# Moving stores of zeros to other places in the order of a backward attention kernel

## The chip, the cores and the metric

The kernel runs on one core of one Trainium2 chip. The metric is device time in microseconds (us); five executions of the kernel before took 283.5 to 284.99 us, with a median of 283.81 us. A sixth execution was profiled.

## What is computed

The program computes one layer's output and all gradients for a decode step: attention over the last 1024 positions of a cache of 4096, beside a gated feed-forward block.

```python
B, Sq, D = 4, 1, 512
Hq, Hkv, Sk, Dh = 32, 8, 4096, 128
W = min(4096, max(256, Sk // 4))          # 1024: only these positions are attended to
k = jnp.repeat(k_cache[:, :, Sk - W:, :], rep, axis=1)
v = jnp.repeat(v_cache[:, :, Sk - W:, :], rep, axis=1)
p = _softmax(jnp.einsum("bhqd,bhkd->bhqk", q, k) * (Dh ** -0.5), axis=-1)
return x + _A_ref(xn, A_k_cache, A_v_cache, A_wq, A_wo) + _B_ref(xn, B_w_gate, B_w_up, B_w_down)
_out, _vjp = jax.vjp(_f, A_x, A_k_cache, A_v_cache, A_wq, A_wo, B_w_gate, B_w_up, B_w_down)
return (_out0, *[jnp.asarray(_g) for _g in _grads])
```

The gradients of the two caches (`out_2` for k, `out_3` for v) have the full shape of 4 x 8 x 4096 x 128. Three quarters of each is zero, because positions 0 to 3071 are not attended to. These zeros have to be written to memory: 2 caches x 32 (batch, head) regions = 64 regions of 768 KB, 50 MB in all, out of 81 MB that the kernel writes.

## The kernel before, in words

The feed-forward block comes first. The eight kv heads then go in four groups of two (`NT = 4`, `t` = 0 to 3). For each group the code makes the scores of k (`scores(t, 0)`), the softmax, the scores dP of v (`scores(t, 1)`), then the gradient of the scores, dS (`softmax_d`), the rows of the output and of dq (`odq`), and sums over the weights (`fin`). While that goes on, the large outputs are made in small pieces from a queue `bg`, of which `tick(n)` takes n: `dvdk(t, 0)` gives 16 pieces of dv, `dvdk(t, 1)` 16 pieces of dk, `dw(t)` the pieces of the weight gradients.

**Pieces and stage tiles.** A piece of dv or dk (lines 532 to 543) is one matmul into PSUM (`kv_ps`, line 537), and a copy of it by ScalarE (line 99) or VectorE (line 101) into a stage tile of 1 MB. Eight pieces (jj = 0 to 7) fill one tile, for one head g; with the eighth the tile is stored, by a DMA that SyncE (SP) issues. So a group has four stage tiles, in the order dv g=0, dv g=1, dk g=0, dk g=1. The pool `stage` has three buffers. The last tile of a group, dk g=1, takes the buffer of that group's first, dv g=0, and its first copy waits until the store of dv g=0 has landed.

**DMA queues.** Stores of results go out in order on SP's queue. Stores of zeros go out on ScalarE's queue (line 311): `zeros(n)` issues a DMA for n regions, at most 4 in one, all from one small tile of zeros. A region is 64 pieces of 12 KB. Each such issue is tied to stand behind the latest copy of ScalarE (lines 312 and 313), so that its place among ScalarE's copies is where the call stands. Loads for group t + 2 go out on GpSimd's queue (`load_next`, lines 291 to 297): first v and k of the group's first head, then `wo`, `wq`, k and v of its second, each as soon as the tile that it replaces has been read.

**Places of the zeros.** `zeros` is called in the feed-forward block (2 and 4 regions, line 751), three times in `scores` of each group (4 each, line 411: in the middle of the second half of k's scores and of both halves of v's), in group 0 also between the two (2, line 768), and in the last two groups after `softmax_d`, whose input dP is then done (4, line 771). The call at line 786 would issue what is left; nothing is left by then. A semaphore that a DMA counts up is shared with earlier DMAs of SP and ScalarE in turn (eight of them), and an issue waits for the DMA that had it before.

Of the kernel before, what the change touches and what calls it, by code (L numbers as in the profile page):

```python
# [18 lines left out]
def kernel(  # L19
# [41 lines left out]
    GP = 2  # L61
    NT = G // GP
# [28 lines left out]
    def evac(out, in_, n, half=False, eng=None):  # L91

        eng = "dve" if half else eng or ("act" if chain else None)
        ca, cd = (190 + n) / 1.2, (120 + (n / 2 if half else n)) / 0.96
        if eng is None:
            eng = "act" if load["act"] + ca <= load["dve"] + cd else "dve"
        load[eng] += ca if eng == "act" else cd
        if eng == "act":
            last.append(nc.scalar.copy(out=out, in_=in_))  # L99
            return last[-1]  # L100
        return nc.vector.tensor_copy(out=out, in_=in_)  # L101

    def store(eng, out, in_, kind, apart):

        d = eng.dma_start(out=out, in_=in_)
        for k in apart:
            tc.declare_no_dep(d.ins, group=k, reason="stores write disjoint parts of the outputs")
        tc.add_to_no_dep_group(kind, d.ins)
        return d
# [166 lines left out]
    def load_w(t):  # L276
        eng = nc.gpsimd if t else nc.sync
        pool = wpool[t % 2]
        wo_t[t] = pool.tile([P, HG, D], BF16, name="wo_sb", tag="wo")
        eng.dma_start(out=wo_t[t][:], in_=wo_v[t])  # L280
        wq_t[t] = pool.tile([P, ND, CW], BF16, name="wq_sb", tag="wq")
        eng.dma_start(out=wq_t[t][:], in_=wq_v[t])

    def load_kv(t, k, g):
        d_, src, nm = ((k_t, A_k_cache, "kb"), (v_t, A_v_cache, "vb"))[k]
        tl = kvpool[(GP * t + g) % (2 * GP)].tile([P, J, Dh], BF16, name=nm, tag=nm)
        (nc.gpsimd if GP * t + g > GP else nc.sync).dma_start(out=tl[:].rearrange("p j d -> p (j d)"),
                          in_=src[:, t * GP + g, K0:Sk, :].rearrange("b (m j) d -> m b (j d)", j=J))
        d_[(t, g)] = tl
# [12 lines left out]
    def zeros(n):  # L302


        zs = ztile[0:P:P // ZP, :]
        while n > 0 and zruns:
            og, r = zruns[0]
            w = min(n, B * G - r, GP * 2)
            zsrc = bass.AP(tensor=zs.tensor, offset=zs.offset, ap=[list(zs.ap[0]), [0, w], [1, ZW]])
            zdst = og.rearrange("b g s d -> (b g) s d")[r:r + w, 0:K0, :].rearrange("r (m j) d -> m r (j d)", m=ZP)  # L310
            z = store(nc.scalar, zdst, zsrc, "zeros", ["rest", "zeros"])
            tc.add_manual_dep(z.ins, last[-1].ins.name,
                              mybir.DependencyInfo(mybir.DependencyClass.NoSync, mybir.DependencyReason.DATA))
            n -= w
            zruns[0][1] += w
            if zruns[0][1] == B * G:
                zruns.popleft()
# [4 lines left out]
    def tick(n):  # L322
        for _ in range(min(n, len(bg))):
            bg.popleft()()
# [57 lines left out]
    def masks(t):  # L382
        for k, nm in enumerate(("do", "q")):
            mr = attw.tile([P, GP, NQ, Dh], BF16, name=nm + "mr", tag=nm + "mr", bufs=1)
            for g in range(GP):
                nc.gpsimd.tensor_tensor(out=mr[:, g], in0=st[t]["r4"][:, k, :].unsqueeze(1).broadcast_to([P, NQ, Dh]),  # L386
                                        in1=msk[:, :, g].unsqueeze(2).broadcast_to([P, NQ, Dh]), op=ALU.mult)
            st[t][nm] = mr
# [137 lines left out]
    def dvdk(t, k):  # L526
        src, mr, og = st[t][("P", "dS")[k]], st[t][("do", "q")[k]], (out_3, out_2)[k]
        nm = ("dv", "dk")[k]
        for g in range(GP):
            held = {}  # L530

            def piece(g, jj, held):
                if jj == 0:
                    held["stg"] = stage.tile([P, NQ, JQ, Dh], BF16, name="stg_" + nm, tag="stg")
                stg = held["stg"]
                mps = ps_w.tile([P, NQ, Dh], FP32, name="kv_ps", tag="w")
                nc.tensor.matmul(mps[:].rearrange("p q d -> p (q d)"), lhsT=src[:, jj, :],  # L537
                                 rhs=mr[:, g].rearrange("p q d -> p (q d)"), start=True, stop=True)
                evac(stg[:, :, jj, :], mps[:], 512)
                if jj == JQ - 1:  # L540
                    store(nc.sync, out=og[:, t * GP + g, K0:Sk, :].rearrange("b (m j) d -> m b (j d)", j=J),
                          in_=stg[:].rearrange("p q j d -> p (q j d)"), kind="rest",
                          apart=["zeros", "rest"])

            for jj in range(JQ):
                bg.append(lambda g=g, jj=jj, held=held: piece(g, jj, held))
# [209 lines left out]
    with tc.tile_pool(name="stage", bufs=3, reuse_waits="tile") as stage, \  # L756
            tc.tile_pool(name="wodd", bufs=1, reuse_waits="tile") as wodd:
        wpool.append(wodd)
        kvpool.append(wodd)
        load_w(1)  # L760
        for k in range(2):
            load_kv(1, k, 1)
        for t in range(NT):
            if t == 0:
                pre(t, {})
            masks(t)
            scores(t, 0, {})
            zeros(2 if t == 0 else 0)
            scores(t, 1, softmax(t))
            d1, d2 = softmax_d(t)  # L770
            zeros(4 if t >= NT - 2 else 0)
            if t + 1 < NT:
                pre(t + 1, {0: [d1], 2: [d2]})
            else:
                tick(2)
                d1()
                tick(6)
                d2()
                tick(2)
            odq(t)  # L780
            fin(t)
            load_next(t)
            tick(len(bg))
            dw(t)
        tick(len(bg))
        zeros(2 * B * G)


        acc_r = kvp.tile([P, 2, ND, B, RB], FP32, name="acc_r", tag="kb")
        nc.vector.tensor_copy(out=acc_r[:], in_=acc[:].unsqueeze(4).broadcast_to([P, 2, ND, B, RB]))  # L790
        fin_ps = []
        for o in range(2):
            f_ps = ps_w.tile([P, ND, P], FP32, name="f_ps", tag="w")
            for c in range(ND):
                nc.tensor.transpose(f_ps[:, c, :], acc_r[:, o, c].rearrange("p b r -> p (b r)"), ident_f[:])
            fin_ps.append(f_ps[:])
        acc_o, acc_d = fin_ps[0].rearrange("p c d -> p (c d)"), fin_ps[1].rearrange("p c d -> p d c")

        def adj(x):
            return x[:].rearrange("p (d c) -> p d c", c=ND)  # L800

        out_b = kvp.tile([P, D], BF16, name="out_b", tag="vb")
        nc.vector.tensor_tensor(out=out_b[:], in0=acc_o, in1=x_b[:], op=ALU.add)
        nc.sync.dma_start(out=out_0.rearrange("b s d -> (b s) d"), in_=out_b[0:P:RB, :])

        s1 = const.tile([P, 1], FP32, name="s1")
        nc.vector.reduce_sum(out=s1[:], in_=acc_d, axis=AX.XY)
        pr = kvp.tile([P, D], FP32, name="pr", tag="vb")
        s2 = const.tile([P, 1], FP32, name="s2")
        nc.vector.tensor_tensor_reduce(out=adj(pr), in0=acc_d, in1=adj(xn_f), scale=1.0, scalar=0.0,  # L810
                                       op0=ALU.mult, op1=ALU.add, accum_out=s2[:])
        nm1 = const.tile([P, 1], FP32, name="nm1")
        nc.vector.tensor_scalar(out=nm1[:], in0=s1[:], scalar1=-1.0 / D, scalar2=None, op0=ALU.mult)
        nm2 = const.tile([P, 1], FP32, name="nm2")
        nc.vector.tensor_scalar(out=nm2[:], in0=s2[:], scalar1=-1.0 / D, scalar2=None, op0=ALU.mult)
        nc.vector.scalar_tensor_tensor(out=adj(pr), in0=adj(xn_f), scalar=nm2[:, 0:1], in1=acc_d,
                                       op0=ALU.mult, op1=ALU.add)
        nc.vector.tensor_scalar(out=pr[:], in0=pr[:], scalar1=nm1[:, 0:1], scalar2=rstd[:, 0:1],
                                op0=ALU.add, op1=ALU.mult)
        dx_b = kvp.tile([P, D], BF16, name="dx_b", tag="kb")  # L820
        nc.vector.tensor_tensor(out=dx_b[:], in0=pr[:], in1=dy_b[:], op=ALU.add)
        nc.sync.dma_start(out=out_1.rearrange("b s d -> (b s) d"), in_=dx_b[0:P:RB, :])
# [30 lines left out]
```

## Time and profile before

| What | Value |
|---|---|
| Median of five executions | 283.81 us |
| Profiled execution | 284.25 us |
| Its span (first to last instruction) | 282.5 us |
| Busy: PE, DVE, ACT, POOL | 76%, 56%, 41%, 20% |
| DMA, mean over the span | 397 GB/s, 112.15 MB |
| Share of ScalarE's queue, SP's queue, GpSimd's queue in the DMA engines' span | 42.3%, 39.0%, 15.2% |
| Stores of zeros: 15 of 3072 KB and 2 of 1536 KB, issue to landing | 19.0 and 18.4 us (median) |
| Stores of dv tiles, 8 of 1024 KB, issue to landing | 19.8 us (median) |

PE is TensorE, DVE VectorE, ACT ScalarE and POOL GpSimd. "SPq" and "ACTq" are the parts of SP and ScalarE that issue DMAs. The share of busy time is a mean over stretches with different limits, so it doesn't say what a change at one place is worth. The chain of waits is followed back from the last instruction to what released each step.

### The profile page before, as it was taken

The page shows a single profiled execution, that of the slowest core. Times are in us where ns is not written, and L with a number is a line of the kernel's source. Part 1 is how long each engine was busy: PE and PEld are TensorE (multiplying, and loading weights), DVE is VectorE, ACT ScalarE, POOL GpSimd, SP SyncE. Part 2 cuts the span into 40 slices and gives each one's busy share as a digit, 9 for nine tenths or more (in the row PEclk, how much of TensorE's full clock was granted, in tenths as well). Part 3 has the DMA queues.
Part 4 walks back from the last instruction along what each step waited for, and adds up shares of the span by engine and source line. Part 5 has one row for each costly group of instructions (what it writes and reads, how often), then busy time and mean ns, then how long its engine had stood idle before and what let it go on. Part 6 is the DMA issues. An engine that isn't in the chain of part 4 may idle for free.

```text
span 282.5 us, 7190 instructions
## 1 busy us (share of the span) xinstructions
PE 215.9 (76%) x3132; PEld 140.5 (50%) x3132; DVE 159.6 (56%) x336; ACT 115.6 (41%) x214; POOL 56.0 (20%) x56
## 2 busy tenths in 40 slices
PE   1978977987769789967894499786954996878950
PEld 0856854745445565534572265444642754526520
DVE  6955644654457557645583237546752465367691
ACT  1321643454336237535421335455303363571550
POOL 3890003130100534020006060110050201102000
PEclk9985997799798999999599559999896699799795
DMA  7999999999999999999999979999999769999995
GB/s 237 442 394 431 426 397 402 409 418 418 425 424 422 424 422 415 419 427 423 428 423 412 400 209 364 430 425 425 425 422 426 314 255 409 434 418 429 422 412 222
DMA packets 19407, 112.15 MB, mean 397 GB/s; under 512 B 1440, under 2 KB 5040, under 8 KB 10416
## 3 DMA queue, kind: packets, MB, share of 16 engines
q10 hardware_dynamic: 4384, 50.34, 42.3%
q1 hardware_dynamic: 12304, 44.58, 39.0%
q0 software_dynamic: 2688, 16.78, 15.2%
q8 instruction: 24, 0.39, 0.5%
q14 instruction: 7, 0.06, 0.0%
HBM read 30.68 MB, written 81.01 MB: 395 GB/s over the span
## 4 chain that ended last, share of the span: by engine, by line
PE 49%; DMA 23%; DVE 17%; ACT 4%; issue 3%; POOL 2%; ACTq 0%; DVEq 0%
DMA out_dram<-stg_dv 18%; PE T_ps L399 10%; PE kv_ps L537 6%; PE S_ps L404 5%; DMA out_dram<-osb_g 5%; PE dwo_ps L556 3%; DVE T_sb L101 3%; PE acc_ps L213 3%; PE wgT_ps L742 3%; PE dwq_ps L568 2%; POOL P_x L417 2%; PE woT_ps L338 2%; PE dwg_ps L715 2%; ACT stg_dk L99 2%; PE wqT_ps L595 2%
## 5 line engine op out<-in xcount | busy, mean ns | idle before, releaser
L101 DVE COPY T_sb<-T_ps 128x1024 bf16<-128x1024 bf16 x64 | 43.8, 690 | 38.3 <-PE T_ps L399 38.0
L99 ACT CAST stg_dk<-kv_ps 128x512 bf16<-128x512 f32 x40 | 22.0, 588 | 52.4 <-PE kv_ps L537 37.1
L99 ACT CAST stg_dv<-kv_ps 128x512 bf16<-128x512 f32 x57 | 30.4, 591 | 30.1 <-PE kv_ps L537 30.1
L537 PE MATMUL kv_ps<-qmr,dS_x 128*128 128x512 bf16 x64 | 22.5, 432 | 14.2 <-ACT stg_dk L99 12.4
L537 PE MATMUL kv_ps<-domr,P_x 128*128 128x512 bf16 x64 | 23.6, 444 | 5.4 <-POOL P_x L417 4.8
L101 DVE CAST stg_dk<-kv_ps 128x512 bf16<-128x512 f32 x24 | 16.1, 686 | 14.5 <-PE kv_ps L537 14.4
L399 PE MATMUL T_ps<-ident,kb 128*128 128x128 bf16 x256 | 24.2, 235 | 0.0
L399 PEld LDWEIGHTS <-kb 128*128 128x128 bf16 x256 | 19.2, 107 | 8.9 <-issue 6.4
L386 POOL TENSOR_TENSOR domr<-r,msk 128x512 bf16<-128x512 bf16 x8 | 8.2, 1041 | 77.0 <-DVE r L379 77.0
L99 ACT CAST osb_g<-dwg_ps 128x512 bf16<-128x512 f32 (+1 forms) x28 | 14.3, 538 | 18.9 <-PE dwg_ps L715 9.4
L399 PE MATMUL T_ps<-ident,vb 128*128 128x128 bf16 x256 | 21.4, 226 | 0.0
L399 PEld LDWEIGHTS <-vb 128*128 128x128 bf16 x256 | 16.6, 102 | 7.2 <-issue 5.6
L99 ACT CAST osb_o<-dwo_ps 128x512 bf16<-128x512 f32 x25 | 14.5, 587 | 10.6 <-PE dwo_ps L556 9.9
L404 PE MATMUL S_ps<-T_sb,dom 128*32 128x256 bf16 x128 | 12.7, 387 | 7.8 <-DVE T_sb L101 7.3
L417 POOL TENSOR_TENSOR P_x<-P_b,bmsk 128x1024 bf16<-128x1024 bf16 x4 | 7.6, 1893 | 54.1 <-ACT P_b L465 54.1
L101 DVE COPY woT<-woT_ps 128x1024 bf16<-128x1024 bf16 x16 | 11.0, 689 | 12.0 <-PE woT_ps L338 12.0
L99 ACT CAST osb_q<-dwq_ps 128x512 bf16<-128x512 f32 x25 | 14.2, 587 | 8.4 <-PE dwq_ps L568 7.8
L595 PEld LDWEIGHTS <-wq_sb 128*128 128x128 bf16 x128 | 9.0, 103 | 14.7 <-issue 13.0
L338 PE MATMUL woT_ps<-ident,wo_sb 128*128 128x128 bf16 x128 | 12.6, 253 | 2.6 <-DVE stg_dv L101 1.9
L338 PEld LDWEIGHTS <-wo_sb 128*128 128x128 bf16 x128 | 10.8, 116 | 7.1 <-issue 6.1
L101 DVE COPY wqT<-wqT_ps 128x1024 bf16<-128x1024 bf16 x16 | 11.0, 688 | 5.6 <-PE wqT_ps L595 5.5
L101 DVE COPY wgT<-wgT_ps 128x1024 bf16<-128x1024 bf16 x14 | 9.7, 692 | 7.6 <-PE wgT_ps L742 7.6
(214 smaller groups left out, 402.6 us busy)
## 6 DMA issues: line engine op xcount, KB each, us to landing
out_dram<-ztile ACTq DMA_DIRECT2D x15, 3072.0 KB, 19.0
out_dram<-stg_dv SPq DMA_DIRECT2D x8, 1024.0 KB, 19.8
out_dram<-stg_dk SPq DMA_DIRECT2D x8, 1024.0 KB, 13.2
kb<-in_A_k_cache_dram POOLq DMA_DIRECT2D x5, 1024.0 KB, 17.8
vb<-in_A_v_cache_dram POOLq DMA_DIRECT2D x5, 1024.0 KB, 25.0
out_dram<-osb_o SPq DMA_DIRECT2D x8, 512.0 KB, 14.0
out_dram<-osb_q SPq DMA_DIRECT2D x8, 512.0 KB, 16.9
out_dram<-osb_g SPq DMA_DIRECT2D x8, 448.0 KB, 15.2
```

Source lines behind the costliest of these rows:

```text
L99: last.append(nc.scalar.copy(out=out, in_=in_))
L101: return nc.vector.tensor_copy(out=out, in_=in_)
L213: nc.tensor.matmul(ps[:, c, :], lhsT=lf(c), rhs=rhs, start=(k == 0), stop=(k == len(terms) - 1))
L338: nc.tensor.transpose(wT_ps[:, i, c, :], wo_sb[:, 2 * h2 + i, c * P:(c + 1) * P], ident[:])
L386: nc.gpsimd.tensor_tensor(out=mr[:, g], in0=st[t]["r4"][:, k, :].unsqueeze(1).broadcast_to([P, NQ, Dh]), in1=msk[:, :, g].unsqueeze(2).bro ...
L399: nc.tensor.transpose(T_ps[:, jj, :], blks[(t, g)][:, q * JQ + jj, :], ident[:])
L404: nc.tensor.matmul(ps[b * RG:(b + 1) * RG, :], lhsT=lf[:, b, s * RG:(s + 1) * RG], rhs=T_sb[:, :, b], start=(g == 0 and q == 0), stop=(g = ...
L417: eng.tensor_tensor(out=dst[:].rearrange("p j (m b) -> p (j m) b", b=B), in0=src[:].unsqueeze(2).broadcast_to([P, WQ, B]), in1=bmsk[:].uns ...
L537: nc.tensor.matmul(mps[:].rearrange("p q d -> p (q d)"), lhsT=src[:, jj, :], rhs=mr[:, g].rearrange("p q d -> p (q d)"), start=True, stop= ...
L556: nc.tensor.matmul(mps[:], lhsT=X[:].rearrange("p h d -> p (h d)")[:, g * rep + i:CW:HG], rhs=dyz[:], start=True, stop=True)
L595: nc.tensor.transpose(wT_ps[:, i, c, :], wq_sb[:, c, h * Dh:(h + 1) * Dh], ident[:])
L742: nc.tensor.transpose(wT_ps[:, i, c, :], wsb[:, c, fc * P:(fc + 1) * P], ident[:])
```

## The change

Stores of zeros are issued in other places. The number of regions is the same, 64. A new call stands where the first piece of dk g=1 takes its stage tile, the tile that waits for dv g=0: 2 regions in group 1 and 3 in group 2. In exchange the call after `softmax_d` issues 2 regions instead of 4 in group 2, and 1 instead of 4 in group 3. There are 19 issues instead of 17.

```diff
             def piece(g, jj, held):
                 if jj == 0:
                     held["stg"] = stage.tile([P, NQ, JQ, Dh], BF16, name="stg_" + nm, tag="stg")
+                    if (k, g) == (1, GP - 1) and 0 < t < NT - 1:
+                        zeros(2 if t == 1 else 3)
                 stg = held["stg"]
...
             d1, d2 = softmax_d(t)
-            zeros(4 if t >= NT - 2 else 0)
+            zeros({NT - 2: 2, NT - 1: 1}.get(t, 0))
             if t + 1 < NT:
                 pre(t + 1, {0: [d1], 2: [d2]})
```

The order of instructions in the built program shows two further things. In groups 1 and 2 the new issue stands on ScalarE's queue between the last copy into dk g=0 and the first copy into dk g=1. And on GpSimd's queue the loads for group 3, which were issued in the order `wo`, `wq`, k, v, now come as `wq`, k, v, `wo`. The orders of TensorE and VectorE and of SP's stores are the same.

## The prediction

> **What bounds the kernel now.** I read the page's rows of DMA throughput first, because 112 MB have to pass.
>
> ```profile
> span 282.5 us, 7190 instructions
> ...
> DMA  7999999999999999999999979999999769999995
> GB/s 237 442 394 431 426 397 402 409 418 418 425 424 422 424 422 415 419 427 423 428 423 412 400 209 364 430 425 425 425 422 426 314 255 409 434 418 429 422 412 222
> ```
>
> A slice is 7.06 us. Where nothing starves it, the DMA moves about 425 GB/s. It has two holes, slices 23 and 24 (162 to 176 us) and 31 and 32 (219 to 233 us); each misses about 0.65 of a slice, 4.6 us. The chain of waits in order of time tells what comes before each hole:
>
> ```profile
> 131.50 27.02 DMA out_dram<-stg_dv
> ...
> 158.61 0.59 ACT stg_dk L99
> ...
> 190.45 24.49 DMA out_dram<-stg_dv
> ...
> 215.04 0.59 ACT stg_dk L99
> ...
> 275.69 0.69 DVE dx_b L821
> ```
>
> Columns are start, us, what. The whole kernel from 131 us on hangs on two landings of a dv tile (at 158.6 and 215.0). After each comes a chain of compute: 31.8 us to the next dv store, and after the second 61.4 us to the last vector instruction (276.4). ScalarE's timeline shows the copies that waited, the last tiles of groups 1 and 2:
>
> ```profile
> 149.80 1.07 ACT L99 CAST stg_dk<-kv_ps 128x512 bf16<-128x512 f32 x2 [3.84 <-PE kv_ps L537]
> 158.61 1.56 ACT L99 CAST stg_dk<-kv_ps 128x512 bf16<-128x512 f32 x3 [7.74 <-DMA out_dram<-stg_dv]
> ...
> 207.57 0.59 ACT L99 CAST stg_dk<-kv_ps 128x512 bf16<-128x512 f32 x1 [3.79 <-PE kv_ps L537]
> 215.04 1.07 ACT L99 CAST stg_dk<-kv_ps 128x512 bf16<-128x512 f32 x2 [6.88 <-DMA out_dram<-stg_dv]
> ```
>
> So ScalarE stands still for 7.74 and 6.88 us. The table by stretches shows the first hole:
>
> ```profile
> 158.00:162.00 4.00, 2.75 (x19) 1.76 (x18) 1.38 (x2) 2.35 (x5) 0.00 (x0) 0.50 0.98 414
> 162.00:166.00 4.00, 3.71 (x76) 3.00 (x76) 1.29 (x5) 0.87 (x2) 2.37 (x5) 0.50 0.44 117
> 166.00:171.00 5.00, 5.00 (x42) 2.81 (x41) 2.67 (x4) 2.80 (x5) 2.07 (x3) 0.69 0.99 277
> 171.00:176.00 5.00, 5.00 (x57) 2.80 (x56) 3.42 (x6) 3.04 (x6) 0.00 (x0) 1.00 1.01 416
> ```
>
> The last three columns are TensorE's granted clock, the DMA's share and GB/s. At the end the stores decide, by SP's timeline:
>
> ```profile
> 271.25 2.34 SPq L105 DMA_DIRECT2D out_dram<-osb_q  x2
> ...
> 276.41 0.54 SPq L822 DMA_DIRECT2D out_dram<-dx_b  x1
> ```
>
> The last vector instruction ends at 276.4, but the trace's last packets of osb_q run until 280.82, and the packets of dx_b, behind them in SP's queue, at 278.8. The span ends 1.66 us after the last packet.
>
> Counting the trace's packets by queue and size gives the prices (16 DMA engines; us of one packet: 12 KB 0.460, 8 KB 0.309, 4 KB 0.159, 2 KB 0.084):
>
> ```
> us               SP 8K/4K/2K    ACT 12K   POOL 8K/4K
> 192 to 196          0/0/118        120       0/0
> 150.9 to 158.6    222/0/2           18     133/0
> 171.15 to 214.94  312/256/512      910     256/130
> 262 to end        311/256/512      204       0/0
> ```
>
> **What the Trainium skill says.** "DMA: Bandwidth & Descriptors", section "Queues, rings and completion order": each DMA engine goes round the queues that have work, a packet from each. The trace agrees: 118 small packets of SP beside 120 of 12 KB from ScalarE in 4 us. A zero that waits beside a store thus costs that store 0.46 us per packet and engine. The same page, "Why a DMA increments its semaphore by 16 and not by 1": a DMA has landed when its slowest engine has. Here by 152 us 116 packets of 8 KB of the 128 of dv g=0 had started, yet it landed at 158.5. "TensorE: Matmul & The Clock Gate", part 1 on the HAM clock gate: the clock halves after an idle window of about 3.4 us. Here it was at half from 213.47 to 223.71, around a pause of 5.92 us, and at full through a pause of 1.81 us at 97.7.
>
> **The change, part by part.**
>
> *Two regions in group 1.* 128 packets, 8 for each engine, issued when ScalarE is free at 150.87. Their semaphore's earlier store, osb_o issued at 114.66, landed at 129.83, so nothing holds the issue. ScalarE's queue still has zeros until about 153, so the new ones follow. On the slowest engine the last osb_q landed at 152.53; from there to 158.5 its 8 packets of dv (2.5 us), about 3 zeros (1.4) and 8 of the loads (2.5) make 6.4 us. Now 8 zeros fit in between, 5 more: 5 x 0.46 = +2.3 us. Bounds: 0.9 if the zeros come only for the last 2 packets, 3.7 if all 8 come on top. I take +2.4: this wait becomes about 10 us, and all that is queued behind the copy (ScalarE's copies, TensorE's PSUM buffers, `fin`, the next scores) starts that much later.
>
> *The loads.* `wq` goes first, as soon as its last transposes are done (160.75 before) instead of behind `wo`'s issue (163.63). With the wait 2.4 longer it is issued at 163.2, the same moment as `wo` before. The load that now comes last, `wo`, is wanted at 191.78 + 2.4 = 194.2; the last load landed at 190.47. If that cover were gone, TensorE's pause of 5.92 us would take it.
>
> *The landing in group 2.* From 171.15 the DMA is never idle. The packets until the landing sum to (312 x 0.309 + 256 x 0.159 + 512 x 0.084 + 910 x 0.46 + 256 x 0.309 + 130 x about 0.25) / 16 = 44.4 us, against 43.8 passed. After: SP's stores come 2.4 us later, at 173.55. The loads have run alone for 2.4 us more, at the 45 packets a us of 166 to 171, so some 108 x 0.309 / 16 = 2.1 us of them are already done. The cut from 4 regions to 2 counts little: of the fourth store of zeros 142 packets had passed before the landing and 128 are left, 14 x 0.46 / 16 = 0.4 us. Landing: 173.55 + 43.8 - 2.1 - 0.4 = 214.8, i.e. -0.2 us. So what the first wait adds, the second gives back: it shrinks from 6.88 to about 4.3. Bounds of this shift: -2.5 to +2.4 (nothing given back).
>
> *Three regions in group 2.* Issued at about 210.6, when ScalarE's queue has packets anyway: none on the landing. Afterwards ScalarE's queue carries one region more than before, 64 x 0.46 / 16 = 1.8 us, into a hole of 4.6 us. Cost nothing; without the hole 1.8. The two added issues (0.61 us each) lie in ScalarE's waits.
>
> *One region for four in group 3.* 192 packets fewer, 192 x 0.46 / 16 = 5.5 us. Up to 262 us ScalarE sent 820 of this group's 1024; now there are 832, so SP has the DMA alone from there. Its own packets cost (311 x 0.309 + 256 x 0.159 + 512 x 0.084) / 16 = 11.2 us, which ends before the compute does. Then dx_b, issued at 276.41, sets the end: first packet 0.86 us later (as osb_o at 226.52, first packet 227.38), 277.3, and 1.66 more, 279.0 instead of 282.5: -3.5 us. Bounds: -2 if osb_q still drains at 277 to 279, -4.
>
> Sum: -0.2 - 3.5 = -3.7. The profiled execution, 284.25 us (1.75 around the span), becomes 280.5; the median lies 0.44 lower: **280.1 us**, its own range 278.5 to 282.
>
> **The rivals.**
>
> *The clock stays up.* If the second wait leaves TensorE less than the idle window (5.92 - 2.6 = 3.3 us), the half clock until 223.7 may not come. Groups of 8 transposes took 0.85 us there against 0.45: some 1.7 us less on the chain, 278.4 us. Against it: the clock was also halved at 135 us without such a pause.
>
> *Nothing given back.* The landing in group 2 moves with its issue: +2.4 - 3.5 = -1.1, 282.7 us, no change. For it: the loads alone, in `wq`'s 2 KB rows, moved 277 GB/s, so the extra time may move less.
>
> *Slower.* At 150.9 us the zeros delay stores and loads together. The first wait takes the full 8 x 0.46 = 3.7; the loads, pushed back as far, run 3.7 us longer beside osb_q, which then goes at 17 instead of 29 packets a us: 44 packets, +1.5 us at the second landing. 283.81 + 3.7 + 1.5 - 3.5 = 285.5 us. It decides once the shift at the second landing passes +4.9. Against it: the hole at 162 to 166, 117 GB/s, takes 3 us of such delay.
>
> That the issue comes too late, behind the waiting copy, is excluded by the program's order.
>
> **How the numbers follow.** Own forecast 0.46, clock 0.20, nothing given back 0.22, slower 0.12. Half a per cent, 1.4 us, is about what a measurement of this kernel can tell from no change: below 282.4 and above 285.2. The first two are faster, and a third of the third (0.07): 0.73. Same 0.15, slower 0.12. The range reaches from 277.0, below the clock's case by a larger tail gain, to 284.5, above the third case by a tail of only -2; beyond it lies mainly the slower case.
>
> **What would show it.** Group 1's wait on stg_dv about 10 us instead of 7.74; group 2's about 4 instead of 6.88; the first hole, 162 to 166, partly filled; the second filled by 1.8 us; the last packets near 277, with dx_b the last. The prediction is wrong if group 2's landing stands above 217, or if osb_q still ends after 280.

## The result and the profile after

The change makes no measurable difference. The kernel before took 284.44 us (median of 71 executions beside the runs below), the changed kernel 285.23 us (median of 36). The ratio is 1.0011, with a 95% interval of 0.9992 to 1.0031. The forecast was 280.1 us, faster. All ratios below are to the kernel before on the same chip and leave disturbed executions out, so they differ slightly from the quotient of two medians.

The changed kernel was profiled twice. The first profiled execution took 286.63 us (before: 284.25). Its page shows that the holes are still there:

```profile
span 284.9 us, 7191 instructions
...
DMA  7999999999999999999999989999999658999965
GB/s 237 435 413 424 422 400 420 406 414 429 424 425 427 421 422 416 425 429 421 423 426 424 419 278 361 427 426 426 427 416 428 273 234 353 422 435 418 421 285 218
```

A slice is now 7.12 us, counted from 0. The first hole (slices 23 and 24: 278 and 361 where before had 209 and 364) is a little shallower. The second (273, 234, 353) has become wider: against 425 GB/s it misses 0.98 of a slice, 7 us, where before missed 4.6. The region more that was forecast for it has not filled it. The chain of waits in order of time (start us, us, what) has the same two landings, both later:

```profile
130.09 32.78 DMA out_dram<-stg_dv
...
162.99 0.70 DVE stg_dk L101
...
195.69 24.75 DMA out_dram<-stg_dv
...
220.53 0.70 DVE stg_dk L101
...
281.54 0.69 DVE dx_b L823
```

The first landing takes 32.78 us from its issue instead of 27.02, and the second 24.75 instead of 24.49: it wasn't shortened. ScalarE's timeline shows the two new issues (ACTq) and the copies that wait:

```profile
148.76 0.61 ACTq L105 DMA_DIRECT2D out_dram<-ztile  x1
149.02 0.59 ACT L99 CAST stg_dk<-kv_ps 128x512 bf16<-128x512 f32 x1
162.97 1.56 ACT L99 CAST stg_dk<-kv_ps 128x512 bf16<-128x512 f32 x3 [13.36 <-DMA out_dram<-stg_dv]
...
211.68 0.63 ACTq L105 DMA_DIRECT2D out_dram<-ztile  x1
220.54 1.56 ACT L99 CAST stg_dk<-kv_ps 128x512 bf16<-128x512 f32 x3 [8.28 <-DMA out_dram<-stg_dv]
```

The waits grew from 7.74 to 13.36 us and from 6.88 to 8.28 us. The stretches around the first hole, in the columns of the table shown of before (the last three are TensorE's clock, DMA share and GB/s):

```profile
158.00:162.00 4.00, 0.00 (x0) 0.00 (x0) 0.00 (x0) 0.00 (x0) 0.00 (x0) 0.50 1.01 421
162.00:166.00 4.00, 1.48 (x10) 1.04 (x10) 1.38 (x2) 1.56 (x3) 0.95 (x2) 0.50 0.82 342
166.00:171.00 5.00, 4.71 (x85) 3.62 (x84) 1.34 (x5) 1.66 (x3) 2.27 (x4) 0.50 0.87 274
171.00:176.00 5.00, 5.00 (x42) 2.87 (x40) 2.41 (x4) 2.57 (x5) 1.19 (x2) 0.62 0.97 338
```

From 158 to 162 us no engine computes, while the DMA moves 421 GB/s. At the end, SP's timeline shows what was forecast:

```profile
277.12 1.50 SPq L105 DMA_DIRECT2D out_dram<-osb_q  x2
...
282.26 0.54 SPq L824 DMA_DIRECT2D out_dram<-dx_b  x1
```

The last packets of the execution are now those of `dx_b`, at 283.56 us; 2.6 us pass from the last vector instruction (282.24) to the end of the span, where before had 6.1 us (276.38 to 282.48).

### The profile page after: what moved, and what is told of

Its sections match the earlier page's. It is cut to its first block, busy times and chain, and to the rows that moved or that the text cites. A ratio compares the mean times of both kernels' runs of the same rounds, so it can differ in the third digit from the quotient of the medians.

```text
span 284.9 us, 7191 instructions
## 1 busy us (share of the span) xinstructions
PE 213.3 (75%) x3132; PEld 138.4 (49%) x3132; DVE 158.9 (56%) x336; ACT 115.5 (41%) x214; POOL 55.9 (20%) x56
## 4 chain that ended last, share of the span: by engine, by line
PE 44%; DMA 29%; DVE 17%; ACT 3%; issue 3%; POOL 2%; ACTq 0%; DVEq 0%; SPq 0%
DMA out_dram<-stg_dv 20%; PE T_ps L399 10%; PE kv_ps L539 7%; PE S_ps L404 6%; DMA out_dram<-osb_d 6%; DVE T_sb L101 4%; DMA out_dram<-ztile 3%; PE dwo_ps L558 3%; PE acc_ps L213 3%; PE dwq_ps L570 2%; POOL P_x L417 2%; PE wqT_ps L597 2%; DVE stg_dk L101 2%; PE wgT_ps L744 1%; DVE wqT L101 1%
## 5 line engine op out<-in xcount | busy, mean ns | idle before, releaser
L597 PE MATMUL wqT_ps<-ident,wq_sb 128*128 128x128 bf16 x128 | 11.0, 230 | 20.4 <-DVE stg_dk L101 17.5
L399 PEld LDWEIGHTS <-kb 128*128 128x128 bf16 x256 | 20.1, 111 | 11.1 <-issue 8.7
L399 PE MATMUL T_ps<-ident,kb 128*128 128x128 bf16 x256 | 25.1, 242 | 0.0
L399 PEld LDWEIGHTS <-vb 128*128 128x128 bf16 x256 | 16.3, 101 | 6.9 <-issue 5.0
L558 PE MATMUL dwo_ps<-dyz,od_x 128*128 128x512 bf16 x32 | 13.6, 461 | 0.2 <-ACT osb_o L99 0.2
```

The source lines that it names most:

```text
L399: nc.tensor.transpose(T_ps[:, jj, :], blks[(t, g)][:, q * JQ + jj, :], ident[:])
L558: nc.tensor.matmul(mps[:], lhsT=X[:].rearrange("p h d -> p (h d)")[:, g * rep + i:CW:HG], rhs=dyz[:], start=True, stop=True)
L597: nc.tensor.transpose(wT_ps[:, i, c, :], wq_sb[:, c, h * Dh:(h + 1) * Dh], ident[:])
```

## The experiments

The "price" of a place below is the ratio of a kernel with zeros there, less the ratio of the kernel that only lacks them at the end. One per cent is 2.84 us. The interval of a difference is worked out as the root of the two squared half widths.

### The end: regions left out

Two regions are taken from group 3's call and never written (`drop2`), or three (`drop3`).

```diff
-            zeros(4 if t >= NT - 2 else 0)
+            zeros({NT - 2: 4, NT - 1: 2}.get(t, 0))     # drop3: NT - 1: 1
...
-        zeros(2 * B * G)
```

> The kernel before with 2 regions fewer after softmax_d of group 3, and these 2 issued nowhere: they stay unwritten, so this is the worth of taking 2 regions out of the end, without the price of another place. Theory (from there the end is set by the store of dx_b): the part from the last vector instruction to the end shrinks from 6.1 to 2.7 us, the waits of groups 1 and 2 stay at 7 to 8: 281 us, ratio 0.985 to 0.991. Rival (the end does not hang on these zeros): ratio 0.996 to 1.002.

> As the kernel with 2 unwritten regions, but with 3 (group 3 issues 1 after softmax_d, as in the changed kernel). Theory: no more is gained than with 2, because dx_b sets the end either way: ratio 0.985 to 0.991, and the gap to the kernel with group 2's call alone, 1.0054, is what 3 regions in group 2 cost, about 1.6%. Rival (each region is worth its DMA time, 1.84 us, since the DMA's total is the bound): 0.65% below the kernel with 2 unwritten regions.

Measured: 0.9855 [0.981, 0.9901] and 0.9854 [0.9807, 0.99]. So emptying the end is worth 1.45%, 4.1 us (forecast: 3.5), and the third region adds nothing to the second. SP's timeline of the kernel with two regions left out ends as that of the changed one does:

```profile
271.45 1.48 SPq L105 DMA_DIRECT2D out_dram<-osb_q  x2
273.09 1.15 SPq L803 DMA_DIRECT2D out_dram<-out_b  x1
276.57 0.54 SPq L821 DMA_DIRECT2D out_dram<-dx_b  x1
```

`dx_b` goes out at 276.57 us, as before (276.41), but the last packet passes at 278.23 instead of 280.82. What is gained here has to be paid for at the place the zeros are moved to.

### Group 1 alone

Only the call in group 1, with two regions, and group 3 short of two; with four regions; and, for the part that the changed order of group 3's loads plays, that order alone. (Both kernels with group 1's call have this order too: `wq`, k, v, `wo`.)

```diff
                     held["stg"] = stage.tile([P, NQ, JQ, Dh], BF16, name="stg_" + nm, tag="stg")
+                    if (k, g) == (1, GP - 1) and t == 1:
+                        zeros(2)                         # g1_four: zeros(4)
...
-            zeros(4 if t >= NT - 2 else 0)
+            zeros({NT - 2: 4, NT - 1: 2}.get(t, 0))     # g1_four: {NT - 2: 4}
```

```diff
-            load_w(t + 2)
+            if t + 2 < NT - 1:
+                load_w(t + 2)
+            else:
+                wq_t[t + 2] = wpool[(t + 2) % 2].tile([P, ND, CW], BF16, name="wq_sb", tag="wq")
+                nc.gpsimd.dma_start(out=wq_t[t + 2][:], in_=wq_v[t + 2])
...
+            if t + 2 == NT - 1:
+                wo_t[t + 2] = wpool[(t + 2) % 2].tile([P, HG, D], BF16, name="wo_sb", tag="wo")
+                nc.gpsimd.dma_start(out=wo_t[t + 2][:], in_=wo_v[t + 2])
```

> Only group 1's new call is kept (2 regions ahead of its last dk tile); after softmax_d group 2 issues 4 as before and group 3 issues 2, so that the sum stays 64 regions. Theory (these zeros stand beside the store of dv that the tile waits for, one packet for one on its slowest engine, and the time is not given back): ScalarE's wait in group 1 is 12 to 13.5 us instead of 7.7, the tail is 3 us shorter, together 285.5 to 288 us, ratio to before 1.004 to 1.012. Rival (the cost lies in group 2's three regions): wait in group 1 about 8 to 10 us and 281 to 282.5 us, ratio 0.988 to 0.994.

> Group 1's new call with 4 regions instead of 2; group 2 as before (4 after softmax_d, no new call); group 3 issues none after softmax_d; 64 in all. Theory (a price for each region ahead of the wait, a gain at the end that does not grow): group 1's wait 13 to 15 us against 10.0 with 2 regions, the end as with 2: 285 to 287 us, ratio 1.001 to 1.008. Rival (regions put into group 1's hole are free): 283 us or less, ratio 0.990 to 0.996.

> The kernel before, with the zeros where they were, but with group 3's loads in the order of the changed kernel: wq, k, v, wo. Theory: TensorE has slack for it and the DMA moves the same bytes, so nothing is gained: waits of 7 to 8 us, 284 to 285 us, ratio 0.997 to 1.003. Rival (the order of the loads, and not the 2 regions, makes the kernel with group 1's call alone faster than before): ratio 0.993 to 0.997.

Measured: 0.9952 [0.9926, 0.9978], 1.0051 [1.0026, 1.0077] and 1.0026 [0.9995, 1.0057]. Two regions here have a price of 0.97 ± 0.52%, 2.8 us (1.3 to 4.2); four cost 1.96%, 5.6 us. The price fits a delay of the forecast's size (+2.4) of which nothing comes back; within its interval it also fits the whole DMA time of the two regions, 3.7 us.

With four regions, half of the 22 executions took 284.6 to 286.4 us, the other half 288.6 to 290.7, and 5.6 us is in the main the price in the first half. The profile is of the second (289.72 us): its first wait is 4.50 us, where 13 to 15 were expected, and TensorE waits 16.9 us for `wo`, the load that this order puts last. So there the cover that the forecast's step on the loads counted on was gone; whether that makes the second half, one profile can't tell.

ScalarE's timeline of the kernel with group 1's call alone shows both waits:

```profile
161.66 1.56 ACT L99 CAST stg_dk<-kv_ps 128x512 bf16<-128x512 f32 x3 [10.02 <-DMA out_dram<-stg_dv]
...
219.04 1.07 ACT L99 CAST stg_dk<-kv_ps 128x512 bf16<-128x512 f32 x2 [7.20 <-DMA out_dram<-stg_dv]
```

The first wait is 10.02 us, as forecast; the second 7.20, and not 4.3. The loads did come earlier: from the first store of `osb_o` in group 2 on, 230 packets of GpSimd's queue were left, against 471 before (3.9 us of DMA time instead of 6.9). But from that store's issue to the waiting copy passed 44.88 us (174.17 to 219.04), against 44.55 before (170.49 to 215.04). With the load order alone it took 45.89 us. The lines are SP's issue of `osb_o` before, the same with group 1 alone, and ScalarE's second wait with the load order alone:

```profile
170.49 3.48 SPq L105 DMA_DIRECT2D out_dram<-osb_o  x2
...
174.17 3.49 SPq L105 DMA_DIRECT2D out_dram<-osb_o  x2
...
216.08 1.07 ACT L99 CAST stg_dk<-kv_ps 128x512 bf16<-128x512 f32 x2 [8.21 <-DMA out_dram<-stg_dv]
```

Why earlier loads brought no earlier landing stands in the semaphore of the dv store. It counts up once for each of the 16 DMA engines, and the trace has the time of each count. The table gives, for group 2's dv g=0, the us from the first store of `osb_o` until 15 engines were done and until all 16 were (the last two rows are kernels told further below):

| Kernel | Order of group 3's loads | 15 engines | all 16 | the last one behind |
|---|---|---|---|---|
| before | `wo`, `wq`, k, v | 43.08 | 44.45 | 1.37 |
| load order alone | `wq`, k, v, `wo` | 40.52 | 45.78 | 5.26 |
| group 1 alone | `wq`, k, v, `wo` | 39.89 | 44.78 | 4.89 |
| changed | `wq`, k, v, `wo` | 38.95 | 44.72 | 5.77 |
| changed, again | `wq`, k, v, `wo` | 41.25 | 44.76 | 3.51 |
| group 1's two behind the wait | `wo`, `wq`, k, v | 42.05 | 43.69 | 1.64 |
| one region in each place | `wq`, `wo`, k, v | 40.04 | 40.85 | 0.81 |

On 15 engines the landing did come earlier, by 1.8 to 4.1 us in the four profiles with the order `wq`, k, v, `wo` (the kernels with the order of before have 42.1 to 44.8 us). One engine was late and took it back. (In the profile with four regions, of the same order, the last engine is 8.0 us behind.) In nine other kernels with the order of before and packets of 12 KB it is 0.8 to 1.6 us. The kernel with the load order alone moves no zeros, so it is this order that goes with the late engine. What in the order makes it late is not shown, nor which engine it is: the counts don't name it.

The same counts tell what group 1's two regions do to the first landing. With them ahead of the wait, 15 engines were done 21.8 to 24.9 us after the issue of dv g=0 (before: 24.0), and the last one 7.2 to 7.9 us behind in three profiles. In the kernels without zeros there and with packets of 12 KB it is 3.0 to 5.4 us behind (0.1 in the kernel with zeros in the feed-forward block), with one region 5.5. The profile with four regions, 2.6, doesn't fit this series.

### Group 2 alone, and the same zeros behind the wait

Three regions in group 2 and none in group 1; one region there, with two left unwritten; three put behind the first waiting copies (third piece, jj = 2) instead of ahead of them; group 1's two put behind likewise, with the other calls as in the changed kernel (the loads keep the order of before); and the cut of group 2's call to two regions by itself, the two left unwritten.

```diff
+                    if (k, g) == (1, GP - 1) and t == 2:
+                        zeros(3)                         # g2_one: zeros(1)
...
+            zeros({NT - 2: 4, NT - 1: 1}.get(t, 0))
```

```diff
                 if jj == 0:
...
+                if (k, g, jj) == (1, GP - 1, 2) and t == 2:   # g2_late
+                    zeros(3)
...
+                if (k, g, jj) == (1, GP - 1, 2) and t == 1:   # g1_late, with zeros(3) at jj == 0 of t == 2
+                    zeros(2)
...
+            zeros({NT - 2: 4, NT - 1: 1}.get(t, 0))           # g1_late: {NT - 2: 2, NT - 1: 1}
+            zeros({NT - 2: 2, NT - 1: 4}.get(t, 0))           # drop_g2, without any other call
...
-        zeros(2 * B * G)                                      # g2_one and drop_g2
```

> Only group 2's new call is kept (3 regions ahead of its last dk tile); after softmax_d group 2 issues 4 as before, group 3 issues 1. Theory: group 1's wait is back at 7 to 8.5 us, group 2's stays at 6 to 8, the tail is 3.4 us shorter: 281 us, ratio 0.986 to 0.991. Rival (group 2's regions delay the landing that is waited for): group 2's wait is 9 us or more, and the time is 283.5 to 285.5, ratio 0.997 to 1.004.

> The kernel before, with one region issued ahead of group 2's last dk tile and one region in group 3; the call after group 2's dP keeps 4 and two regions stay unwritten, so that only the first region in the hole is priced. Theory that DMA work sets the landings and the hole is already used up by stores that run ahead: one region costs its full 1.84 us, ratio 0.992. Theory of the prediction, that a first region fits into the hole: nothing, 0.9855 as with two regions unwritten and none added.

> As the kernel with group 2's call alone (3 regions there, 1.0054), but they are issued with the third piece of the last dk tile, behind the copies that wait for the landing. Theory (it is the DMA work that they add before group 3's landing, not their place beside the waited store): group 3's wait on its dv tile is again 3 to 5 us, ratio 1.002 to 1.008. Rival (they cost by standing beside the store that group 2 waits for): ratio 0.986 to 0.994.

> As the changed kernel, but group 1's 2 regions are issued with the third piece of the last dk tile, i.e. behind the copies that wait instead of ahead of them. Theory (it is the place ahead of the wait that costs): group 1's wait 7 to 8.5 us, the hole after it partly filled, the tail 3.4 us shorter: 280 to 282 us, ratio 0.984 to 0.992. Rival (1.5 MB more before group 2's landing cost 3.7 us of DMA there, wherever they are put): group 2's wait 9 to 11 us and 283.5 to 285.5 us, ratio 0.997 to 1.004.

> The kernel before with 2 regions fewer after softmax_d of group 2, issued nowhere (2 regions stay unwritten); group 3 issues 4 as before. The prediction put this cut at 0.4 us. Theory (the landing of group 2 is set by the packets that pass before it, and these 2 regions mostly pass after it, into the hole): ratio 0.997 to 1.002. Rival (each region taken out is worth its DMA time of 1.84 us, as each one added in group 2 cost): ratio 0.985 to 0.990.

| Kernel | Ratio [95%] | Price of its place |
|---|---|---|
| three in group 2 | 1.0054 [1.0022, 1.0086] | 2.0%, 5.7 us |
| one in group 2, two unwritten | 0.9883 [0.985, 0.9917] | 0.3 ± 0.6%, 0.8 us |
| three in group 2, behind the wait | 1.0029 [1.0002, 1.0055] | 1.75%, 5.0 us |
| changed kernel, group 1's two behind the wait | 1.0001 [0.9974, 1.0027] | as ahead of it (1.0011) |
| group 2's call cut to two, unwritten | 0.9991 [0.996, 1.0021] | nothing gained |

One region costs 0.8 us here, with an interval (-0.8 to 2.4) that holds both nothing and its DMA time of 1.84; three cost about as much as their whole DMA time, 192 packets of 0.46 us on 16 engines, 5.5 us. Behind the waits the regions cost about the same as ahead of them, in group 1 as in group 2, so the price is not only that of standing beside the store that is waited for. With group 1's two behind the wait the first two waits are 7.22 and 6.20 us; the third is 3.53. The page of the kernel with three in group 2 shows that the hole was filled (slices 31 and 32: 425 and 379):

```profile
GB/s 236 443 396 429 423 398 369 408 390 429 428 423 422 426 418 425 421 429 425 419 428 410 392 197 363 426 423 431 423 419 428 425 379 431 408 433 419 330 220 233
```

ScalarE's timeline shows who paid. The first line is of the kernel before, the others are of the kernel with three in group 2:

```profile
260.44 0.59 ACT L99 CAST stg_dk<-kv_ps 128x512 bf16<-128x512 f32 x1 [0.59 <-DMA out_dram<-stg_dv]
...
216.41 1.56 ACT L99 CAST stg_dk<-kv_ps 128x512 bf16<-128x512 f32 x3 [7.13 <-DMA out_dram<-stg_dv]
...
265.83 0.59 ACT L99 CAST stg_dk<-kv_ps 128x512 bf16<-128x512 f32 x1 [4.38 <-DMA out_dram<-stg_dv]
```

Group 3 has a wait on a dv tile too. Before it was 0.59 us; here it is 4.38. A count of packets from the second landing to the first zeros of group 3 (by size; work is their time summed over 16 engines) tells how the hole is used:

```
kernel             us               SP 8K/4K  ACT 12K  work us   of us
before             214.94 to 229.74  328/128    114      11.0     14.8
three in group 2   216.31 to 232.28  324/76     299      15.7     16.0
one in group 2     215.02 to 230.98  329/128    176      12.8     16.0
changed            220.44 to 235.44  213/125    120       8.9     15.0
changed, again     219.20 to 235.22  230/128    119       9.2     16.0
group 1 alone      218.95 to 233.70  233/128     49       7.3     14.8
```

With three regions no idle time is left, 52 packets of 4 KB of SP's stores are pushed beside group 3's own zeros, and the third landing comes 16.3 us after its issue (249.41 to 265.73) instead of 12.6 (247.82 to 260.4). Here too it is one engine: 15 were done 11.6 us after the issue (before 11.5), and the last 4.8 us behind them (before 1.0). The wait grew by 3.8 of the 5.7 us; where the rest lies is not shown. With one region the hole stays open and the end is that of the kernel without it: last vector instruction at 276.72 us, against 276.55.

In the changed kernel 120 zeros were left after the second landing, against 114 before: of its 17 regions up to there (1088 packets) 968 had passed, against 910 of 1024. But with group 1 alone 975 of 1024 had passed and only 49 were left. In both, by the table of engines above, stores and zeros ran ahead on the engines that were not late. Against group 1 alone, the region more that the changed kernel issues is in the hole (71 packets).

### The same two regions elsewhere

Group 1's two regions moved to group 0's last dk tile (`g0_two`), or into the feed-forward block, whose first call takes 4 instead of 2 (`ffn_two`).

```diff
+                    if (k, g) == (1, GP - 1) and t == 0:
+                        zeros(2)
...
-                zeros(4 if og is out_7 else 2)
+                zeros(4)
...
+            zeros({NT - 2: 4, NT - 1: 2}.get(t, 0))     # both
```

> The two regions taken from the end of group 3 stand ahead of group 0's last dk tile; all 64 are written. Theory that a region costs its DMA time wherever the DMA is busy until the next landing: 2 x 1.84 = 3.7 us against 4.1 gained, 0.997 to 1.000. Theory that group 1's place is dear only because its wait stands right behind it: here the next wait is a group away, the regions drain in the holes between, 0.986 to 0.992.

> The two regions taken from the end of group 3 are issued in the feed-forward block, whose first call takes 4 instead of 2; all 64 are written. If the DMA has slack there (its first 30 us move under 400 GB/s in places) the regions cost 0 to 1 us, 0.986 to 0.989. If it has none and loads of the heads come later by it, 3.7 us, 0.998.

Measured: 1.002 [0.9991, 1.0048] and 1.0194 [1.0139, 1.0248]: prices of 1.65 ± 0.54%, 4.7 us, and 3.4 ± 0.7%, 9.6 us, for 3.7 us of DMA time. With the zeros in group 0, dv of group 1 was issued at 135.25 us; in the kernels that are the same as before up to there this was between 129.6 and 133.6. In the feed-forward block the zeros stand beside the stores of `osb_d`, whose buffers the next results want; ScalarE's timeline of that kernel:

```profile
47.90 1.46 ACT L99 CAST osb_g<-dwg_ps 128x512 bf16<-128x512 f32 x3 [5.22 <-DMA out_dram<-osb_d]
62.72 1.84 ACT L99 CAST osb_g<-dwg_ps 128x512 bf16<-128x512 f32 x4 [13.37 <-DMA out_dram<-osb_d]
```

In the profile of before no copy of `osb_g` waited for `osb_d`; in others that are the same up to there such waits reach 3.9 us (three in group 2). The GB/s row here has a hole of its own (168 and 314 in slices 9 and 10), which would explain why the price exceeds the DMA time: work that stands still issues no stores.

### Shorter packets of zeros

If a zero delays a store by one packet in each turn of an engine, shorter packets should delay it less. `small_zeros` is the kernel before with packets of 6 KB; `mid_zeros` has 8 KB, `mid_zeros_g1` also group 1's call.

```diff
-    ZP = P // 2
+    ZP = P                                  # mid_zeros: ZP = 96
...
-        zs = ztile[0:P:P // ZP, :]
+        zs = ztile[0:ZP, :]                 # mid_zeros
```

> The kernel before with one line changed: the tile of zeros is laid over 128 partitions instead of 64, so that a packet of zeros is 6 KB instead of 12 KB; places and sizes of all stores are the same. Theory (each engine takes a packet from each queue in turn, so a store of results pays for one packet of zeros with each of its own): a packet of zeros costs 0.23 us instead of 0.46, the landings that groups 1 and 2 wait for come some 7 us earlier, both waits are 0 to 2 us, and the time is 270 to 274 us, where the DMA's own total holds it; ratio 0.950 to 0.965. Rival (the queues share by bytes or by time): waits as before, 283 to 286 us, ratio 0.997 to 1.005.

> The kernel before with the tile of zeros laid over 96 partitions: packets of 8 KB (0.309 us) instead of 12 KB; places unchanged. From the kernel with 6 KB packets we know that both waits go, and that ScalarE then waits 12.5 us for earlier zeros, which have fallen behind. Theory (each store packet pays for one packet of zeros, so 518 and 640 packets pay 0.15 us less on each of 16 engines before the two landings): the waits shrink by 5 and 6 us to 1 to 3, zeros fall behind less, so that ScalarE waits little for them, and the DMA's total of some 274 us sets the end: 278 to 281.5 us, ratio 0.978 to 0.991. Rival (what the stores gain the zeros lose, and ScalarE's waits for zeros take it all): ratio 0.996 to 1.004.

> Packets of 8 KB together with group 1's call alone (2 regions ahead of its last dk tile, 2 after softmax_d in group 3). Theory (the end and the waits are separate gains): another 0.3 to 0.6% below the kernel with 8 KB packets alone, ratio 0.973 to 0.988. Rival (the DMA's total is all that counts once the waits are short, so a place changes nothing): the same ratio as with 8 KB packets alone, within 0.3%.

Measured: 0.9953 [0.9892, 1.0014], 1.3019 [1.2912, 1.3125] and 1.2967 [1.2885, 1.3049]. With 6 KB the first wait is gone and the second is 1.63 us, as turns packet by packet would have it. The trace of before shows such turns: from 192 to 204 us, 383 times a packet of zeros starts 80 to 90 ns after one of 2 KB, the time of that packet, while the steps of 10 ns around have 60 to 155. But other waits take their place. A copy of `osb_g` waits 10.30 us for `osb_d` (until 60.30), and later, in ScalarE's timeline:

```profile
206.35 1.64 ACT L99 CAST stg_dk<-kv_ps 128x512 bf16<-128x512 f32 x3 [1.63 <-DMA out_dram<-stg_dv]
...
225.53 2.05 ACT L99 CAST osb_q<-dwq_ps 128x512 bf16<-128x512 f32 x4 [6.37 <-DMA out_dram<-ztile]
...
235.38 0.51 ACT L465 ACTIVATE P_b<-E_f,rr 128x256 bf16<-128x256 f32 x1 [6.18 <-DMA out_dram<-ztile]
```

ScalarE's issue of zeros now waits for earlier zeros, whose semaphore it takes over, and holds the copies behind it. The page shows how little room was left:

```profile
GB/s 232 442 400 425 422 401 416 420 422 255 411 412 420 416 386 404 326 420 423 418 423 418 425 422 420 424 421 421 420 420 424 421 419 421 415 426 416 422 328 21
...
q10 hardware_dynamic: 8480, 50.34, 42.8%
q1 hardware_dynamic: 12304, 44.58, 38.9%
q0 software_dynamic: 2688, 16.78, 14.7%
q8 instruction: 24, 0.39, 0.5%
```

From slice 17 to 37 the DMA never moves less than 415 GB/s. The queues' shares (the last number of each line) add up to 96.9% of the engines' span (before 42.3 + 39.0 + 15.2 + 0.5 = 97.0%, 274 us). An estimate from these shares: without faster transfers no order of them gets this kernel much under 274 us, and the fastest execution of all runs took 279.1. The forecast of 270 to 274 us left the new waits out. The kernels with 8 KB are another matter, told at the end.

### Once more, and the best of it

The changed kernel again, unedited; one region in each of the two places; and one region alone in group 2, from group 3.

```diff
+                    if (k, g) == (1, GP - 1) and 0 < t < NT - 1:   # one_in_g2: t == 2
+                        zeros(1)
...
+            zeros({NT - 2: 4, NT - 1: 2}.get(t, 0))                # one_in_g2: NT - 1: 3
```

> The changed kernel once more, unedited, beside the three others: the ratio 0.999 to 1.004 again. For its profile: if the first wait of 13.36 us in the first profile belongs to the change, it is 10 to 14 us again; if it was chance of that execution, about 10.

> One region ahead of the last dk tile in group 1 and one in group 2, 4 and 2 after dP in groups 2 and 3; all 64 are written. If prices add and the first region in group 2's hole is free: end -1.45%, group 1 +0.49% (half of what two cost), group 2 nothing: 0.990, better than the 0.995 with both regions in group 1. If every region costs its 1.84 us wherever it is put: 0.9985. If the first region in group 2 has a price between, 0.993.

> One region alone is moved, from the end of group 3 to the place ahead of group 2's last dk tile; all 64 are written. If the end gives half for one region and the hole takes it free: 0.993. If the end gives the whole 1.45% with the first region, 0.986 to 0.988. If the hole takes nothing free, 0.999.

Measured: 1.0009 [0.998, 1.0037], 0.9924 [0.9894, 0.9954] and 0.9958 [0.9938, 0.9977]. The second profile of the changed kernel (285.24 us) has waits of 10.37 and 7.18 us:

```profile
161.99 1.56 ACT L99 CAST stg_dk<-kv_ps 128x512 bf16<-128x512 f32 x3 [10.37 <-DMA out_dram<-stg_dv]
...
219.30 1.56 ACT L99 CAST stg_dk<-kv_ps 128x512 bf16<-128x512 f32 x3 [7.18 <-DMA out_dram<-stg_dv]
```

So 3 of the 13.36 us were that execution's. Kernels whose program is the same as before up to there show first waits between 7.1 (the load order alone) and 13.4 us (three in group 2 behind the wait); one profile can't settle 2 us at this place, and the ratios decide.

One region in group 2, with nothing moved in group 1, gains 0.42 ± 0.2%. That lies between the 0.993 of a place that costs nothing and the 0.999 of one at full DMA time.

One region in each place, 282.35 us, is faster than before by 0.76% and than the changed kernel by 0.85 ± 0.4% (its ratio against 1.0009). The prices add up to it: -1.45 + 0.49 (half of group 1's two) + 0.28 = -0.68%. Its chain of waits and ScalarE's timeline:

```profile
131.54 29.00 DMA out_dram<-stg_dv
...
193.28 20.87 DMA out_dram<-stg_dv
...
276.41 0.69 DVE dx_b L823
```

```profile
160.64 1.56 ACT L99 CAST stg_dk<-kv_ps 128x512 bf16<-128x512 f32 x3 [9.83 <-DMA out_dram<-stg_dv]
214.25 1.56 ACT L99 CAST stg_dk<-kv_ps 128x512 bf16<-128x512 f32 x3 [4.40 <-DMA out_dram<-stg_dv]
```

Here the second wait did shrink, to 4.40 us, and from `osb_o` to the waiting copy passed 40.95 us, against 43.6 to 46.0 in the other kernels with 12 KB packets whose copy waits there. This kernel differs in one thing more than its zeros: group 3's loads come in a third order, `wq`, `wo`, k, v, and no engine is late at this landing (0.81 us, in the table above). Not all of it reached the end: from this copy to the last vector instruction passed 62.9 us instead of 61.3, with a third wait of 2.13. It is one profile.

## Why the prediction was wrong

In ratios, the way from before to the changed kernel has three terms, in us at 1% = 2.84: the end -4.1 (two regions left out); group 1's two regions +2.8 (group 1 alone, less that); and all the rest, group 2's three regions and cut and one region fewer at the end, +1.7 (changed kernel less group 1 alone: 1.0011 - 0.9952 = 0.59 ± 0.33%). Unrounded they make up the +0.3 us of the ratio by construction. The forecast had -3.5, -0.2 and 0, so most of the miss, 3 us, lies in the middle term.

**The end: right.** -3.5 was forecast with bounds of -2 to -4, and -4.1 measured (2.8 to 5.4). `dx_b` sets the end, as the step said, and the third region taken away added nothing.

**Two regions in group 1: right for the first wait.** The step said +2.4, about 10 us, because more zeros stand before the last packets on the slowest engine. The waits were 10.02, 10.37 and 13.36 us in three profiles with the two regions there. The waits alone don't show it, since they reach 13.4 without any zeros there. The last engine does: 7.2 to 7.9 us behind the others, against 3.0 to 5.4 and one of 0.1. The price of 2.8 us fits too. But put behind the wait the same two regions left the time where it was (1.0001 against 1.0011), with the loads in the order of before. So the shorter first wait of that kernel, 7.22 us, did not help.

**The landing in group 2: wrong, the step that failed.** "So what the first wait adds, the second gives back" was to bring 2.6 us. From the first store of `osb_o` to the copy behind the landing the forecast had 42 us; it took 44.55 us before, and 44.82, 44.85 and 44.88 us in the two profiles of the changed kernel and in that with group 1 alone. The premise held: 218 to 230 packets of loads were left instead of 471. What failed is the sum of packets over 16 engines. It tells when the work is done on average, but a DMA has landed when its slowest engine has, as the forecast itself had quoted from the Trainium skill ("DMA: Bandwidth & Descriptors", section "Why a DMA increments its semaphore by 16 and not by 1"). The trace agrees: 15 engines were done 1.8 to 4.1 us earlier than before, and the last came 3.5 to 5.8 us behind them instead of 1.4. On the others later work ran ahead: in the changed kernel 427 packets of 8 KB of SP's and 968 zeros passed up to the landing, against 312 and 910, 2.2 and 1.7 us of DMA time. The late engine came with the order of group 3's loads, which the step on the loads had weighed only for when `wo` is wanted: that order alone shows it, and the kernel with one region in each place, whose order is another, doesn't. Why this order makes one engine late stays open. The rival "nothing given back" had this outcome (-1.1; end and group 1 together measured -1.4), but not its reason: it doubted that the loads would move faster, and they did.

**The cut from 4 to 2: not contradicted.** 0.4 us was forecast; with the two regions unwritten 0.3 ± 0.9 us was measured.

**Three regions in group 2: wrong.** "Cost nothing; without the hole 1.8" counted 64 packets more into a hole of 4.6 us. Alone, three regions cost 5.7 us, and the third wait, 0.59 us before, grew to 4.38: the step looked no further than the hole, and the next landing had no room. In the changed kernel, with the cut, the net is one region, and by the ratios it cost 1.7 us (0.7 to 2.6). Where, the profiles don't show: the copies behind both landings and the issue of `dx_b` stand within 0.4 us of each other in the second profile of the changed kernel and in that with group 1 alone, and the third wait is 0.61 us.

**Rivals.** The clock stayed down: it was at half from 215.77 to 229.42 us, around a pause of TensorE of 5.90 us, since the second wait did not shrink. With one region in each place, where it did, the pause was 1.83 us, and the clock was at half from 213.29 to 223.53 all the same. So the shorter wait did not keep the clock up there. The slower case, 285.5 us, is near the measured median by its number, but its cause, loads that push back group 2's stores by 1.5 us at the second landing, was not seen: the interval from `osb_o` grew by 0.3.

What the whole sum left out is that the DMA had little slack: before, its engines had work for 97% of the span, which leaves 8.5 us idle by that estimate. Zeros moved into idle time are free only as far as the next landing that something waits for is not pushed back.

## What to carry to other kernels

Where transfers fill 97% of the span, price a moved transfer first at its whole DMA time, whether it stands ahead of a wait or behind it, and count on a hole for little: here one region of 1.84 us cost 0.8 ± 1.6 us in a hole of 4.6 us, and three cost 5.7. Measure the two ends of a move apart (leave the work out, then put it in the new place), since a good end and a dear place cancel in the total; the best split of those tried was one region in each place, 0.9924. Don't forecast a landing from the sum of packets over the engines. Look in the trace how far the last engine is behind the others, and mind that the order of loads on a third queue can change it: here from 1.4 to 5.3 us.

## What the hardware showed beyond that

Zeros read from 96 consecutive partitions, in packets of 8 KB, made the kernel 30% slower, with the same bytes. The page of that kernel (first of the two, an execution of 382.9 us; queue: packets, MB, share):

```profile
DMA packets 21455, 112.15 MB, mean 294 GB/s; under 512 B 1440, under 2 KB 5040, under 8 KB 10416
...
q10 hardware_dynamic: 6432, 50.34, 43.7%
```

The mean is 294 GB/s, where before had 397. A packet of zeros took 309 ns at the median, as an 8 KB packet of the stores does, but 716 ns at the 90th percentile (before: 460 and 466.5 for 12 KB; with 6 KB 234 and 239), with a mean of 433. 6144 packets x 124 ns / 16 = 48 us of the 99 us that the span grew is time within packets of zeros. No run tells whether the number of partitions, their being neighbours or the rows of 8 KB in memory is the cause. A store to a queue that was empty also came slowly beside busy ones: the first packet of zeros issued at 113.32 us (changed kernel) passed at 117.2, and of those issued at 173.69 (before) at 177.59, 3.9 us later, where the forecast had counted 0.86 us from a quiet stretch.
